# Order of set-up work in a fused attention and feed-forward block: constants behind the first layer norms, two weight loads behind the first keys, and one half of a down product in each phase

## The chip, the cores and the metric

The kernel runs on one core of a Trainium2 chip. The metric is the device time of one execution in microseconds (us), as a median over runs. Times inside an execution are counted from the start of the profiled span. The engines are PE (TensorE: matmuls; PEld is its weight load), DVE (VectorE), ACT (ScalarE), POOL (GpSimd) and SP (SyncE, which here only issues DMAs). SBUF is the memory on the core, PSUM the eight banks into which PE accumulates.

## What is computed

A transformer block on x of 2048 tokens by 448: layer norm, attention with 16 heads of 28 in a sliding window of 256, an output projection, a residual; then layer norm, a gated feed-forward part of width 1792, and a residual.

```python
q, k, v = layernorm(x) @ wqkv          # 16 heads of 28
p = softmax(where(0 <= i - j < 256, q @ k.T * 28 ** -0.5, -1e9))
h = x + (p @ v) @ wo
n = layernorm(h)
out = h + (gelu(n @ w_gate) * (n @ w_up)) @ w_down
```

## The kernel before

**Precision.** Matrix products of projections, values, output and feed-forward are made from float32 values split into a high half (rounded to the matmul's own float32 form) and a low half (the rest). One product tile is eleven matmuls, listed in TERMS: seven with the high half of the weights (against high and low halves of the tokens), four with the low half. `to_hi` (line 318, ACT) and `to_lo` (line 321, DVE, sometimes POOL) make the halves; lines 318 and 321 of the profile are these two helpers, so a piece is known by its tiles: `xT` for normed, transposed tokens, `proj` for weight tiles and for the halves of projected queries and keys, `wos` for wo, `rk` and `rq` for keys and queries as the scores read them.

**Who sets the order.** Nothing is scheduled by a compiler. `Lists.op` records every piece of work with its engine, a planned cost and latency, a key (its due time) and what it reads and writes; `after` adds pieces that it must wait for. `Lists.run` then plays the whole kernel through in planned time: at each step every engine takes, among the pieces that could start at once, the one with the smallest key, and the pieces are issued in that order. So each engine's queue is a fixed list, worked off in order on the chip, and one changed key or wait moves pieces everywhere behind it. Pieces with `port=True` on DVE and POOL are kept from overlapping in the plan.

**Opening.** `start` (line 420) loads four tiles of 128 tokens, the value weights of the first half (`wv_load(0)`), the first two weight tiles of queries and keys (`wqk_load`), the other twelve token tiles, and two more weight tiles. It makes the constants: `e8` and from it the picks (four pieces of `rk`, lines 474 to 480), zeros in rows 64 to 95 of `rq` and `rk` (lines 468 to 472), which two SBUF to SBUF copies repeat for the second block (lines 481 and 484), the mask (`const_mask`, line 449), and ones beside the values. `layer_norms` (line 333) makes per tile statistics on DVE (348, 350), a small chain on POOL (339 to 345), the norm `xn` on ACT (363), a transposition on PE (368) into a bank, then the high (318) and low (321) half of `xT`. `values` (line 504; matmuls in line 509) and `project_tile` (line 532; matmuls in 543) follow. While PE would idle early in the plan, `idle` puts in transpositions of `ident` that nobody reads (line 1041).

**Queries and keys** go through DRAM: the high and low half of a projected tile are made in one of two pairs of buffers (`pk`), stored by SP (lines 553 and 555), and loaded again in another layout by `loads` (line 575) for each block B of four query tiles and four heads. Scores are made twice: once for the row maxima (592, DVE 596), then, with the maxima as extra rows, for the exponentials (663, ACT 667); POOL cuts them to the window (678), PE weighs the values (697), and `drain` and `output` (741) finish. `wo_weights` (line 747) loads a part of wo into one raw buffer, splits it on ACT and POOL; it is called for both halves of a half of the heads as soon as the first projections are recorded. `wv_load(1)` loads the second half of the value weights.

**Feed-forward.** There are 56 products n, one per part of 128 of the width and per 512 tokens, in groups of 3, 4, 4 and 3 parts. The first four run as whole matmuls (869). From n = 4 on (PAIRED) a product runs in two phases of ten and eleven pairs of matmuls; a pair uses the upper and the lower half of PE's rows at the same time (845), and in the second phase the halves change sides. Between the phases a word of the bank is read by ACT (`seen`, line 851), which keeps PE from writing the bank too early. Then come gelu on ACT (907), the multiplication on DVE (909) and the halves of the result. The down product of n is also made in two halves of six pairs each, `down_a` and `down_b`, with two more such words behind `down_a`. At the end of a group DVE adds four banks to the residual (940). The order on PE is written out at the end of `feed_forward` (lines 822 to 835): four halves first, then phases and halves alternate.

## Time and profile before

| what | value |
|---|---|
| time, median of 3 runs | 742.24 us (741.76 to 743.04) |
| time of the profiled execution | 741.5 us |
| its span in the profile | 739.8 us |
| instructions | 15325 |
| bytes moved by DMA | 79.46 MB |
| paired feed-forward matmuls from xT and one weight record (L845) | 656 for 94.4 us, 393 ns each |
| projections (L543) | 308 for 97.3 us, 399 ns each |

Busy time of an engine is a share of the span; matmuls are pipelined, so their own durations overlap and a busy PE can still wait a little at each start. A row of a timeline gives start, duration, engine, line, operation, tiles and count, and in brackets the idle time before it and what ended it. A row with a count covers several instructions of one kind and the short gaps between them. A row of stretches gives for each engine busy time and count, the granted clock of PE, DMA's share and GB/s.

### The profile page before, as it was taken

The page shows a single profiled execution, that of the slowest core. Times are in us where ns is not written, and L with a number is a line of the kernel's source. Part 1 is how long each engine was busy: PE and PEld are TensorE (multiplying, and loading weights), DVE is VectorE, ACT ScalarE, POOL GpSimd, SP SyncE. Part 2 cuts the span into 40 slices and gives each one's busy share as a digit, 9 for nine tenths or more (in the row PEclk, how much of TensorE's full clock was granted, in tenths as well). Part 3 has the DMA queues.
Part 4 walks back from the last instruction along what each step waited for, and adds up shares of the span by engine and source line. Part 5 has one row for each costly group of instructions (what it writes and reads, how often), then busy time and mean ns, then how long its engine had stood idle before and what let it go on. Part 6 is the DMA issues. An engine that isn't in the chain of part 4 may idle for free.

```text
span 739.8 us, 15325 instructions
## 1 busy us (share of the span) xinstructions
PE 727.5 (98%) x5908; PEld 650.4 (88%) x5908; DVE 400.1 (54%) x1055; ACT 362.9 (49%) x929; POOL 154.2 (21%) x248
## 2 busy tenths in 40 slices
PE   8999999999999999999999999999999999999997
PEld 7787878888888787778899999999999999999996
DVE  8767977776677878848954413224433132223323
ACT  6657777667666888876643322223422122222221
POOL 5402544353344556463000000000000000000000
PEclk9999999999999999999999999999999999999999
DMA  9996536655565787516750200000100000001102
GB/s 280 260 306 204 169 121 200 192 184 158 166 184 179 185 237 204 134 42 177 166 162 1 87 38 1 1 2 1 42 2 1 1 1 2 1 1 51 51 1 101
DMA packets 83191, 79.46 MB, mean 107 GB/s; under 512 B 34126, under 2 KB 72974, under 8 KB 83086
## 3 DMA queue, kind: packets, MB, share of 16 engines
q1 hardware_dynamic: 83118, 78.48, 36.6%
q8 instruction: 46, 0.75, 0.4%
q14 instruction: 27, 0.22, 0.1%
HBM read 48.23 MB, written 29.36 MB: 105 GB/s over the span
## 4 chain that ended last, share of the span: by engine, by line
PE 88%; DVE 4%; ACT 3%; DMA 2%; issue 1%; SPq 1%; POOL 0%; DVEq 0%; ACTq 0%
PE bank L845 51%; PE bank L543 8%; PE bank L663 6%; PE bank L592 6%; PE bank L697 5%; PE bank L509 4%; PE bank L741 4%; PE bank L869 2%; DMA xT<-xn 1%; DVE bnst L348 1%; ACT pp L667 1%; DMA hres<-in_x_dram 1%; DVE xT L321 1%; ACT xn L363 1%; ACT xT L318 1%
## 5 line engine op out<-in xcount | busy, mean ns | idle before, releaser
L667 ACT ACTIVATE pp<-bank 128x384 f32<-128x384 f32 (+2 forms) x352 | 121.9, 389 | 52.1 <-PE bank L663 48.3
L596 DVE CUSTOM_DVE_ANT_0 mt<-bank,mt 128x384 bf16<-128x384 f32 (+2 forms) x256 | 127.6, 525 | 35.3 <-PE bank L592 33.0
L909 DVE TENSOR_TENSOR mt<-bank,mt 128x512 f32<-128x512 f32 x54 | 37.2, 690 | 169.7 <-ACT mt L907 169.5
L907 ACT ACTIVATE mt<-bank 128x512 f32<-128x512 f32 x54 | 32.1, 594 | 144.9 <-PE bank L845 144.9
L678 POOL TENSOR_SCALAR_AFFINE_SELECT pp<-pp 128x512 f32<-128x512 f32 x120 | 75.8, 644 | 126.5 <-ACT pp L667 122.4
L663 PE MATMUL bank<-rq,rk 104*128 104x384 f32 (+2 forms) x352 | 96.8, 304 | 1.4 <-ACT rq L318 0.7
L543 PE MATMUL bank<-xT,proj 128*128 128x512 f32 x308 | 97.3, 399 | 0.2 <-DVE bnmv L350 0.2
L845 PE MATMUL bank<-xT,rec 64*128 64x512 f32 x656 | 94.4, 393 | 0.0
L845 PE MATMUL bank<-xT,rk 64*128 64x512 f32 x656 | 91.3, 388 | 0.0
L845 PEld LDWEIGHTS bank<-xT,rec 64*128 64x128 f32 x656 | 81.1, 184 | 2.6
L845 PEld LDWEIGHTS bank<-xT,rk 64*128 64x128 f32 x656 | 79.5, 184 | 2.0
L592 PE MATMUL bank<-rk,rq 84*128 84x384 f32 (+2 forms) x256 | 81.0, 342 | 0.0
L663 PEld LDWEIGHTS bank<-rq,rk 104*128 104x128 f32 x352 | 64.3, 189 | 17.7 <-ACT pp L667 3.8
L851 ACT ACTIVATE word<-bank 1x1 f32<-1x1 f32 x162 | 25.8, 160 | 99.4 <-PE bank L845 96.4
L845 PE MATMUL bank<-xT,proj 64*128 64x512 f32 x533 | 72.7, 388 | 0.0
L845 PEld LDWEIGHTS bank<-xT,proj 64*128 64x128 f32 x533 | 63.0, 184 | 2.5 <-ACT word L851 0.4
L543 PEld LDWEIGHTS bank<-xT,proj 128*128 128x128 f32 x308 | 55.9, 189 | 6.3 <-ACT proj L318 0.4
L509 PE MATMUL bank<-proj,xT 128*128 128x224 f32 x352 | 59.7, 278 | 0.5 <-ACT xT L318 0.2
L845 PE MATMUL bank<-rk,proj 64*128 64x448 f32 x384 | 57.6, 362 | 0.0
L321 DVE TENSOR_TENSOR proj<-mt,proj 128x512 fp32r<-128x512 f32 x54 | 37.4, 692 | 35.7 <-ACT proj L318 35.6
L845 PE MATMUL bank<-rec,proj 64*128 64x448 f32 x360 | 54.3, 364 | 0.0
L509 PEld LDWEIGHTS bank<-proj,xT 128*128 128x128 f32 x352 | 52.3, 191 | 2.1 <-ACT xT L318 0.5
(114 smaller groups left out, 1155.6 us busy)
## 6 DMA issues: line engine op xcount, KB each, us to landing
rk<-k SPq DMA_DIRECT2D x44, 336.0 KB
rq<-q SPq DMA_DIRECT2D x32, 336.0 KB
q<-proj SPq DMA_DIRECT2D x16, 448.0 KB
k<-proj SPq DMA_DIRECT2D x12, 448.0 KB
raw<-in_ffn_dram SPq DMA_DIRECT2D x7, 736.0 KB
v<-in_ffn_dram SPq DMA_DIRECT2D x7, 736.0 KB
hres<-in_x_dram SPq DMA_DIRECT2D x16, 224.0 KB
q<-proj SPq DMA_DIRECT2D x16, 224.0 KB
```

The costliest lines, as they stand in the source:

```text
L321: (eng or nc.vector).tensor_sub(dst, src, f(hi))
L509: op("pe", mm(224), 0.29, key + a / 16, lambda a=a, h=h, wb=wb, xb=xb: nc.tensor.matmul(bank[b.k][:, 0:224], xT[:, xb, t * 128:(t + 1) * 1 ...
L543: op("pe", mm(512) + 0.002, 0.403, key, lambda a=a, h=h, wb=wb, xb=xb: nc.tensor.matmul(bank[b.k], wqk[i][:, h, wb, :], xT[:, xb, c * 512: ...
L592: nc.tensor.matmul(bank[b.k][:, o:384], rq[u][0:3 * DH, j, i * 128:i * 128 + 128], rk[u][0:3 * DH, j, m0 * 128:(i + 3) * 128], start=True, ...
L596: nc.vector.tensor_tensor_reduce(junk[s % 2][:, o:384], bank[b.k][:, o:384], mask[:, o:384], 1.0, -BIG, OP.add, OP.max, mx[i // 2][:, i % ...
L663: nc.tensor.matmul(bank[b.k][:, 0:n], rk[u][0:104, j, m * 128:m * 128 + 128], rq[u][0:104, j, lo * 128:(hi + 1) * 128], start=True, stop=True)
L667: nc.scalar.activation(pp[:, j, o * 128:o * 128 + n], bank[b.k][:, 0:n], AF.Exp, scale=SCALE)
L678: nc.gpsimd.affine_select(a, a, pattern=[[0, 4], [-cm, 128]], compare_op=op_, fill=0.0, base=0, channel_multiplier=cm)
L697: nc.tensor.matmul(bank[b.k][32 * j:32 * j + DH + 1, lo * 128:(hi + 1) * 128], v[:, 4 * c - 2 + m, g % 2, j, :], pp[:, j, at[m] * 128:(at[ ...
L845: nc.tensor.matmul(bank[bk.k][:, 0:n], w, m, start=bool(start), stop=bool(stop), tile_position=(64 * x, 0), skip_group_check=True)
L907: op("act", 0.485 + table, 0.608 + table, key + NP, lambda: nc.scalar.activation(blocks(g2), src(0), AF.Gelu_apprx_tanh), held[0], G2, bs[ ...
L909: op("dve", 0.605, 0.702, key + 2 * NP, lambda: nc.vector.tensor_tensor(blocks(g2), src(1), blocks(g2), op=OP.mult), [*G2, *held[1]], G2, ...
```

## The change

1. Constants. The zeros of `rk` and `rq` on POOL, the four picks, the two copies and the mask move from `start` into a function `constants`, called when the first four tiles' norms are recorded. All but the copies (which depend on the others) wait for the last piece of the fourth tile's norm, the low half of its `xT`.
2. Loads. `wo_weights` of the first half of the heads, and `wv_load(1)`, wait for the last load of block 1's keys. `wo_weights` is called after the loads of the second block of a half instead of before those of the first.
3. Down halves. Behind every phase of a product there is now one half of a down product. Before, there were two behind the first phase of product 4 alone, and from there on one.

```diff
-    def dma(key, size, fn, r=(), w=(), cost=0.44):
-        return op("sp", cost, 0, key, fn, r, w, size=size)
+    def dma(key, size, fn, r=(), w=(), cost=0.44, after=()):
+        return op("sp", cost, 0, key, fn, r, w, size=size, after=after)
...
         for t in ts:
             normalise(t, key(t), kind)
+            marks["xT", t] = L.ops[-1]
...
+    def constants(after):
...
-        op("pool", 1.35, 1.4, -99, lambda: nc.gpsimd.memset(f(rk_m[64:96, 0:1536]), 0.0), (), [("zk", 0, 0)], port=True)
-        op("pool", 0.95, 1.0, -98, lambda: nc.gpsimd.memset(f(rq_m[64:96, 1024:2048]), 0.0), (), [("zq", 0, 1)], port=True)
+        op("pool", 1.35, 1.4, -99, lambda: nc.gpsimd.memset(f(rk_m[64:96, 0:1536]), 0.0), (), [("zk", 0, 0)], port=True, after=after)
+        op("pool", 0.95, 1.0, -98, lambda: nc.gpsimd.memset(f(rq_m[64:96, 1024:2048]), 0.0), (), [("zq", 0, 1)], port=True, after=after)
...
                 op("dve", 0.55, 0.54, -96 + j, lambda j=j, src=src: nc.vector.tensor_copy(rk[0][96:104, j], src),
-                   ["e8"], [("pick", 0, j)], port=True)
+                   ["e8"], [("pick", 0, j)], port=True, after=after)
...
-        op("pool", 1.0, 1.0, -18, const_mask, (), ["mask"], port=True)
+        op("pool", 1.0, 1.0, -18, const_mask, (), ["mask"], port=True, after=after)
...
     def wv_load(p, key):
         for i in range(2):
             dma(key, 224, lambda i=i: nc.sync.dma_start(wv_raw[p][:, 2 * i:2 * i + 2], wv_in[p][:, 2 * i:2 * i + 2]),
-                (), [WVRAW(p, 2 * i, 2)])
+                (), [WVRAW(p, 2 * i, 2)], after=[got[HOLDV]] if p else ())
...
             get(1, c, i, 2, 2 + i, key + 4 * i)
+        got[B] = L.ops[-1]
...
-        dma(key - 20, 224, lambda: nc.sync.dma_start(wo_raw, wo_in[g]), (), [WORAW])
+        dma(key - 20, 224, lambda: nc.sync.dma_start(wo_raw, wo_in[g]), (), [WORAW], after=[got[HOLDO]] if g < 2 else ())
...
             for ph in phase[m]:
-                order.append(ph)
-                for _ in range(2 if ph is phase[PAIRED][0] else 1):
-                    order.append(todo.pop(0))
+                order += [ph, todo.pop(0)]
...
+                if c == 0:
+                    constants([marks["xT", 3]])
...
             if c == 0:
                 if not p:
                     clear()
-                wo_weights(2 * p)
-                wo_weights(2 * p + 1)
             for B in (8 * p + 2 * c, 8 * p + 2 * c + 1):
                 loads(B)
+                if B % 8 == 1:
+                    wo_weights(2 * p)
+                    wo_weights(2 * p + 1)
```

`HOLDO` and `HOLDV` are 1. The first zeros of `rq` (DVE, line 468), those of `rk` on ACT (471), `e8`, `ident` and the ones stay in `start`.

More of the change, by code (lines that the diff above doesn't have):

```diff
@@ L45 @@
 SOON = 2
+HOLDO = 1
+HOLDV = 1
 PAIRED = 4
@@ L330, in block_kernel @@
     NP = len(TERMS)
+    marks = {}
     def layer_norms(ts, key, kind):
@@ L354, in layer_norms @@
         for t in ts:
+            marks["ve", t] = L.ops[-1]
+        for t in ts:
             normalise(t, key(t), kind)
+            marks["xT", t] = L.ops[-1]
     def normalise(t, key, kind):
@@ L468, in start, with const_mask @@
         op("dve", 1.1, 1.15, -99, lambda: nc.vector.memset(f(rq_m[64:96, 0:1024]), 0.0), (), [("zq", 0, 0)])
[L469 to L470 removed]
         op("act", 1.45, 1.55, -97, lambda: nc.scalar.activation(
             rk_m[64:96, 1536:3072], e8[64:96, 0:1].to_broadcast([32, 1536]), AF.Copy), ["e8"], [("zk", 0, 1)])
+        op("pool", 0.9, 0.95, -10, lambda: nc.gpsimd.memset(v[:, :, :, :, DH:DH + 1], 1.0), (), ["ones"])
+        wv_split(0)
+    def constants(after):
+        def const_mask():
+            nc.gpsimd.memset(mask, 0.0)
+            nc.gpsimd.affine_select(mask[:, 0:128], mask[:, 0:128], pattern=[[1, 128]], compare_op=OP.is_gt,
+                                    fill=-BIG, base=0, channel_multiplier=-1)
+            nc.gpsimd.affine_select(mask[:, 256:384], mask[:, 256:384], pattern=[[-1, 128]], compare_op=OP.is_ge,
+                                    fill=-BIG, base=0, channel_multiplier=1)
+        op("pool", 1.35, 1.4, -99, lambda: nc.gpsimd.memset(f(rk_m[64:96, 0:1536]), 0.0), (), [("zk", 0, 0)], port=True, after=after)
+        op("pool", 0.95, 1.0, -98, lambda: nc.gpsimd.memset(f(rq_m[64:96, 1024:2048]), 0.0), (), [("zq", 0, 1)], port=True, after=after)
         for j in range(4):
@@ L476, in start @@
                 op("dve", 0.55, 0.54, -96 + j, lambda j=j, src=src: nc.vector.tensor_copy(rk[0][96:104, j], src),
-                   ["e8"], [("pick", 0, j)], port=True)
+                   ["e8"], [("pick", 0, j)], port=True, after=after)
             else:
                 op("act", 0.75, 0.85, -96 + j, lambda j=j, src=src: to_hi(rk[0][96:104, j], src), ["e8"],
-                   [("pick", 0, j)])
+                   [("pick", 0, j)], after=after)
         dma(-20, 246, lambda: nc.sync.dma_start(f(rk_m[84:104, 3072:6144]), f(rk_m[84:104, 0:3072])),
@@ L485, in start @@
             [("zq", 0, i) for i in range(2)], [("zq", 1, i) for i in range(2)])
-        op("pool", 1.0, 1.0, -18, const_mask, (), ["mask"], port=True)
-        op("pool", 0.9, 0.95, -10, lambda: nc.gpsimd.memset(v[:, :, :, :, DH:DH + 1], 1.0), (), ["ones"])
-        wv_split(0)
+        op("pool", 1.0, 1.0, -18, const_mask, (), ["mask"], port=True, after=after)
     def wv_load(p, key):
@@ L563, in block @@
         return 2 * p + r % 2, r // 2
+    got = {}
     def loads(B):
```

6 lines of the change are left out of this document (removed).

## The prediction

> **What bounds the kernel now.** I read the page first (busy shares, slices, the chain that ended last), then PE's timeline, then those of the other engines where PE is not dense.
>
> ```profile
> PE 727.5 (98%) x5908; PEld 650.4 (88%) x5908; DVE 400.1 (54%) x1055; ACT 362.9 (49%) x929; POOL 154.2 (21%) x248
> PE   8999999999999999999999999999999999999997
> DMA  9996536655565787516750200000100000001102
> PE 88%; DVE 4%; ACT 3%; DMA 2%; issue 1%; SPq 1%; POOL 0%; DVEq 0%; ACTq 0%
> ```
>
> PE is the bound: 98% busy, 88% of the chain. 98% of 739.8 us leaves 12.3 us idle, so no change that leaves the matmuls alone can win more than those plus unneeded PE work. The one loose slice is the first, and there the DMA queue is full (the first three slices, 55 us, read 9). So I looked at the opening.
>
> ```profile
> 2.13 5.12 PE L1041 MATMUL bank<-ident 128*128 128x128 f32 x25 [2.13 <-POOL ident L443]
> 8.20 0.66 PE L368 MATMUL bank<-ident,xn 128*128 128x128 f32 x4 [0.95 <-ACT xn L363]
> 11.66 1.25 PE L509 MATMUL bank<-proj,xT 128*128 128x224 f32 x9
> 13.54 1.69 PE L509 MATMUL bank<-proj,xT 128*128 128x224 f32 x13
> 15.10 1.13 PE L509 MATMUL bank<-proj,xT 128*128 128x224 f32 x8
> 16.07 5.17 PE L543 MATMUL bank<-xT,proj 128*128 128x512 f32 x22
> ...
> 30.53 0.66 PE L368 MATMUL bank<-ident,xn 128*128 128x128 f32 x4 [0.66 <-ACT xn L363]
> 32.34 0.66 PE L368 MATMUL bank<-ident,xn 128*128 128x128 f32 x4 [0.38 <-ACT xn L363]
> ...
> 39.05 0.34 PE L592 MATMUL bank<-rk,rq 84*128 84x128 f32 x2
> ```
>
> Useful work starts with the first transposition at 8.20; the 25 L1041 before it only keep PE going. Values (L509) start at 11.66, projections at 16.07 after 9+13+8 = 30 value products, scores at 39.05. PE loses 0.66 and 0.38 us to late norms near 31.
>
> **The change part by part.** Matmuls, DMAs and vector work are the same in number; the changed program has only 18 L1041 fewer (26 for 44). Everything else is order.
>
> ```profile
> 1.99 2.88 DVE L476 CAST rk<-e 8x768 fp32r<-8x768 f32 x2
> 4.90 0.63 DVE L348 BATCH_NORM_STATS2 bnst<-hres 128x6 f32<-128x448 f32 x1
> ...
> 14.45 1.76 DVE L321 TENSOR_TENSOR xT<-bank,xT 128x384 fp32r<-128x384 f32 x4
> ...
> 17.14 0.59 DVE L348 BATCH_NORM_STATS2 bnst<-hres 128x6 f32<-128x448 f32 x1
> ...
> 20.19 0.59 DVE L348 BATCH_NORM_STATS2 bnst<-hres 128x6 f32<-128x448 f32 x1
> 20.81 0.69 DVE L321 TENSOR_TENSOR proj<-bank,proj 128x512 fp32r<-128x512 f32 x1
> ...
> 22.75 1.27 DVE L321 TENSOR_TENSOR proj<-raw,proj 128x512 fp32r<-128x512 f32 x2
> ```
> ```profile
> 2.77 1.68 POOL L469 MEMSET rk<- 32x1536 f32 x1
> 5.92 0.23 POOL L339 TENSOR_SCALAR bnve<-bnmv 128x1 f32<-128x1 f32 x1 [0.17 <-POOL rq L470]
> ```
> ```profile
> 6.92 0.58 ACT L318 ACTIVATE proj<-pp 128x448 fp32r<-128x448 f32 x1 [1.45 <-DMA pp<-in_wv_dram]
> 7.40 0.74 ACT L363 ACTIVATE xn<-hres,bnve 128x448 f32<-128x448 f32 x1
> ```
> ```profile
> 0.00:4.00 4.00, 1.87 (x9) 1.87 (x10) 2.92 (x3) 3.17 (x4) 3.06 (x15) 1.00 0.52 141
> 0.00:6.00 6.00, 3.87 (x18) 3.87 (x19) 4.86 (x6) 4.64 (x5) 4.90 (x17) 1.00 0.67 187
> ```
>
> *1. Constants leave the head.* Now DVE's two picks (to 4.87) delay the first statistics to 4.90, and POOL's memsets delay L339 to 5.92 (its releaser is L470). The tile was there sooner: the stretch to 4.00 moved 4 x 141 = 564 KB (the last column is GB/s), and a tile has 229. So I start the first statistics at 3.4 instead of 4.90. Behind them it took 5.92 - 4.90 = 1.0 to POOL, 1.5 to the norm (7.40) and 0.8 to PE (8.20): now POOL about 4.3 (no memset in the way), the norm 5.6, the first transposition 6.4. The fourth tile gains less: four tiles are 917 KB, and the stretch to 6.00 moved 1122, so it lands near 5.5 and its statistics end about 0.6 earlier. From 6.92 ACT and DVE bound: ACT alternates weight halves, norms and high halves of xT at 0.5 to 0.65 us each, and DVE makes four low halves of 0.88 (1.76 for two tiles) and three of 0.6 in between. DVE can start at about 9.1 (6.92, three pieces of ACT and the first high half's own 0.6) and ends at 9.1 + 4 x 0.88 + 3 x 0.6 = 14.4; before, the 1.76 us from 14.45 end at 16.2. PE then starts values near 10.3 and, with 33 of them at 0.12 (1.69 for 13, less the last one's tail) and 0.5 for a transposition, projections at 14.8. That is 1.3 earlier than 16.07 with three more values done (0.35): **1.6 us ahead**.
>
> *2. They come back behind tile 3.* The constants now wait for the last low half (14.4). On POOL two memsets (1.68 for the larger) and the mask stand in front of the next norms, some 4 us; PE wants those only behind 40 projections and 14 values more, at 25: covered. On ACT two picks lie in a wait for PE: covered. On DVE it is tight. Behind 14.4 the changed order has both picks, seven statistics (20.19 - 17.14 over four: 0.76 each), two low halves of projections (0.69) and then the low half of the third weight tile (1.27 for two: 0.64). A pick alone is unknown: 1.44 each in the row, but they ran beside POOL's memsets, and the second ended at 4.87, 0.42 behind the larger memset (2.77 + 1.68). If it stood still until then, a pick takes 0.42. Bounds 0.42 and 1.44; I take 0.55, since the changed order puts POOL's and DVE's pieces mostly one behind the other. 14.4 + 1.1 + 5.3 + 1.4 + 0.64 = 22.85. PE reaches the first product that needs it (the eighth of its tile) at 14.8 + 29 x 0.23 (5.17 for 22) + 0.35 = 21.8 and waits 1.05. Before, that half was ready at 22.75 + 0.64 = 23.4 and PE did not wait. So 0.55 of the lead is left, plus the values: **0.9**. With picks of 1.44 it is 24.6, and 0.9 is lost instead.
>
> [...]
>
> *3. Loads moved behind the keys.*
>
> ```profile
> 12.74 0.91 SPq L481 DMA_DIRECT2D rk<-rk  x1
> ...
> 24.36 0.89 SPq L493 DMA_DIRECT2D raw<-in_wv_dram  x2
> ...
> 26.29 0.92 SPq L750 DMA_DIRECT2D raw<-in_wo_dram  x1
> ```
> ```profile
> 31.04 0.60 ACT L318 ACTIVATE proj<-bank 128x512 fp32r<-128x512 f32 x1 [0.57 <-DMA k<-proj]
> ```
>
> Now two loads of values and one of wo stand on SP (1.8 us of issue) between the stores of the first keys and their loads, in a full queue. ACT waits at 31.04 for such a store to land, the norms wait behind it, and PE loses the 0.66 + 0.38 quoted, with small change 1.3. The changed order has the fifth tile's transposition earlier and no such load among the stores. Against it, the copy rk<-rk, issued at 12.74 now, can go only after the second pick, about 19.5, straight in front of the first store. I take 0.3 of the stalls as left: **1.0 gained**; 1.3 at best, a loss of 1.0 if that copy holds the first store. Scores follow at about 37 instead of 39.05. The moved loads then fall into the fourth slice, where DMA has room (6). Their splits are not free.
>
> ```profile
> 24.27 1.16 POOL L321 TENSOR_TENSOR wos<-raw,wos 128x448 fp32r<-128x448 f32 x1 [1.96 <-ACT wos L318]
> ```
>
> This and its twin now stand among POOL's mask selections of the first block, 1.16 each; values wait for these. Bounds 0 and 2.3; nearer nothing, since PE has projections to do: **0.3 lost**.
>
> *4. One half of a down product per phase.*
>
> ```profile
> 354.51 1.59 PE L845 MATMUL bank<-rq,proj 64*128 64x448 f32 x12 [1.05 <-ACT word L851]
> ```
>
> At one place both halves of a down product stand back to back, and the second waits for ACT's one-word read of the first, itself late behind ACT's queue: 1.05 us idle. A phase of the next product, 22 matmuls, now stands between. What is late next is the word of the phase before, read by the same ACT queue with one half as cover instead of two: I allow 0.15. **0.9 gained**, bounds 0 and 1.05.
>
> Sum: 0.9 + 1.0 - 0.3 + 0.9 = **2.5 us**. In the profiled execution 741.5 (1.7 more than its span) becomes 739.0; the median of the runs shown is 0.74 higher, so 742.24 becomes **739.7**. Between 40 and 340 us the order of PE's rows is shuffled, with waits of tenths either way: plus or minus 1.
>
> **The rivals.** *A. DVE does not bind* (statistics overlap better than 0.76): 1.6 + 1.3 + 1.05 - 0.3 = 3.65, 738.6. Against it: the four statistics from 17.14 to 20.19 keep that pace with nothing between them.
>
> *B. The lead is given back*: long picks (-0.9), stalls as now (0), -0.3, +0.9: about 742.5, no change that a measurement can tell (under 0.2%, 1.5 us). For it: the pick's row, and the copy in front of the stores.
>
> *C. Slower: the wait moves to group ends.* There the four additions (L940) now come at the end of a product, in front of its multiplication.
>
> ```profile
> 621.62 0.69 DVE L909 TENSOR_TENSOR mt<-bank,mt 128x512 f32<-128x512 f32 x1 [5.16 <-ACT mt L907]
> ...
> 624.92 2.22 DVE L940 TENSOR_TENSOR hres<-bank,hres 128x448 f32<-128x448 f32 x4 [1.21 <-PE bank L845]
> ```
> ```profile
> 622.35 0.63 ACT L318 ACTIVATE proj<-mt 128x512 fp32r<-128x512 f32 x1
> 624.57 0.16 ACT L851 ACTIVATE word<-bank 1x1 f32<-1x1 f32 x1 [1.58 <-PE bank L845]
> ```
> ```profile
> 620.20 0.36 PE L845 MATMUL bank<-rk,proj 64*128 64x448 f32 x1
> ...
> 623.70 0.36 PE L845 MATMUL bank<-rk,proj 64*128 64x448 f32 x1
> ...
> 624.91 0.39 PE L845 MATMUL bank<-xT,proj 64*128 64x512 f32 x1
> ...
> 625.32 0.36 PE L845 MATMUL bank<-rk,proj 64*128 64x448 f32 x1
> ```
>
> The additions start 1.22 after their half (623.70). That half now stands where 620.20 is: 621.42 + 2.22 + 0.69 + 0.63 = 624.96. ACT's order has the high half in front of the word, so the word ends at 625.1 instead of 624.73, and the next phase, which started at 624.91, about 0.4 late. Fifteen group ends: 6 us, 745.7. Against it: the other half of the array is behind anyhow (it still runs the down product at 625.32, so its phase starts at about 625.5), which absorbs 0.4; it decides only if the word ends beyond about 625.3.
>
> *D. PE stays at half speed longer.* The 25 of the first row take 0.2 each, later ones less (13 values in 1.69). If fewer of them leave the clock low until about 16, 6 us of work doubles in price: 3.1 lost, 742.8. [...]
>
> **How the numbers follow.** Forecast 0.48; A 0.20; B 0.17; C 0.07; D 0.05; shuffled waits on the wrong side 0.03. The range goes from A with 1 us of shuffle and no loss at the wo splits, 737.3, to D, 742.8, and leaves out C. Faster by over 0.2% (under 740.8): the forecast nearly whole and A, 0.66; within: B and D nearly whole, and the forecast's edge, 0.24; slower: C and the rest, 0.10.
>
> **What would show it.** First statistics at 3.4, first transposition at 6.4, first projection near 14.8, a wait of PE for DVE's low half at 21.8 to 22.9, the first score at 37, no idle of 1.05 at the third product's second half, words behind high halves at group ends without idle time of PE. I am wrong if PE waits longer at 22, if the first stores land later than the copy lets them, or if a product's cycle grows.

## The result, and the profile after

| kernel | median | lowest to highest | runs |
|---|---|---|---|
| before | 742.08 us | 740.49 to 743.79 | 8 |
| changed | 744.35 us | 743.43 to 745.86 | 8 |

The ratio is 1.0032, 95% interval 1.0018 to 1.0046: the change makes the kernel 2.3 us slower. The forecast was 739.7, with a range to 742.8. The profiled execution took 743.81 us over a span of 742.1, against 741.5 over 739.8.

The page of the changed kernel, first, third and seventh of its busy lines, then the chain that ended last:

```profile
PE 727.5 (98%) x5890; PEld 652.2 (88%) x5890; DVE 398.7 (54%) x1055; ACT 364.7 (49%) x929; POOL 154.4 (21%) x248
PE   8999999999999999999999999999999999999997
DMA  8797556665656788615840210000100000001002
PE 89%; ACT 3%; DVE 3%; DMA 2%; issue 1%; SPq 0%; DVEq 0%; ACTq 0%
```

PE is busy exactly as long as before, 727.5 us, though it issues 18 transpositions fewer. So by the page the whole difference is idle time of PE, a few tenths at many places, and the page cannot show where. PE's timeline can (lines of the changed kernel are 2 to 14 higher than before; L375 is the transposition, L519 the values, L553 the projections, L605 the scores):

```profile
6.37 1.12 PE L375 MATMUL bank<-ident,xn 128*128 128x128 f32 x4
...
15.20 5.17 PE L553 MATMUL bank<-xT,proj 128*128 128x512 f32 x22
20.21 0.49 PE L519 MATMUL bank<-proj,xT 128*128 128x224 f32 x3
20.54 4.57 PE L553 MATMUL bank<-xT,proj 128*128 128x512 f32 x18
...
28.01 0.66 PE L375 MATMUL bank<-ident,xn 128*128 128x128 f32 x4 [0.65 <-ACT v L320]
29.14 0.65 PE L375 MATMUL bank<-ident,xn 128*128 128x128 f32 x4 [0.48 <-ACT xn L370]
...
32.38 0.66 PE L375 MATMUL bank<-ident,xn 128*128 128x128 f32 x4 [0.45 <-ACT xn L370]
...
38.05 0.22 PE L605 MATMUL bank<-rk,rq 84*128 84x128 f32 x1
```

The opening came as forecast up to 25 us: first transposition 6.37 (6.4), first projection 15.20 (14.8; before 16.07). Then three waits of 0.65, 0.48 and 0.45 stand between 28 and 33, where before had 0.66 and 0.38, and the first score comes only 1.0 earlier.

To compare whole stages I added up, over PE's matmuls, the time from one start to the next beyond the shortest that a matmul of that shape shows in the traces. This is PE's lost time; it shows what waits of under 0.2 us add up to, and is good to some 0.3 us, since a few records are missing. From the profiled executions, in us:

```
stage               20-55   55-100   100-345   345-400
before               4.62     5.30     21.08      1.70
changed              5.15     6.95     20.63      2.18
```

The changed kernel loses 0.5 us more in the opening, **1.65 more between 55 and 100**, and 0.5 more at the start of the paired feed-forward; between 100 and 345 it is 0.45 better, and from 360 on the two run alike. About 0.25 of the last two differences comes from where the stages are cut: one wait of PE for DVE stands at 344.90 in the kernel before and at 346.39 in the changed one. That is 2.2 us more, of which the lead at 20 us (about 1.1) covers half: the last matmul ends 1.5 us later (737.3 against 735.9; 0.4 of it these sums do not find). Another 0.8 us lies behind it: the span ends 4.75 us behind the last matmul instead of 3.93. In the experiments below that end took 3.9 to 4.8 us, and 4.7 to 4.8 in three of them (e5, e7, e10); what sets it is not shown.

PE's own waits from 38 to 345 us name the middle stage (columns: total, times, longest), before and then changed:

```profile
PE bank L663 <- ACT rq L318: 0.7, 1, 0.7
PE bank L663 <- ACT pp L667: 0.3, 1, 0.3
```
```profile
PE bank L605 <- DVE mx L609: 1.5, 3, 0.7
PE bank L676 <- ACT rq L320: 0.7, 1, 0.7
```

PE now waits 1.5 us for row maxima of DVE, which it never did before. The reason is beside those waits, in the timelines of DVE and POOL in the changed kernel:

```profile
74.09 1.27 DVE L625 TENSOR_SCALAR mhl<-mx 128x8 fp32r<-128x8 f32 x1
82.46 0.63 DVE L628 SCALAR_TENSOR_TENSOR mhl<-mx,mhl 128x8 fp32r<-128x8 f32 x1
```
```profile
74.06 1.28 POOL L323 TENSOR_TENSOR ohl<-oT,ohl 128x512 fp32r<-128x512 f32 x1 [0.32 <-ACT ohl L320]
82.44 0.64 POOL L691 TENSOR_SCALAR_AFFINE_SELECT pp<-pp 128x512 f32<-128x512 f32 x1 [1.27 <-ACT pp L680]
```

`mhl` is the small piece of DVE (8 columns) that negates the maxima; alone it lasts 0.17. Here it lasts 1.27 and 0.63: it starts 0.02 to 0.03 us behind a long piece of POOL and ends when that ends (74.06 + 1.28 = 75.34; 74.09 + 1.27 = 75.36). The kernel's plan keeps such pieces (`port=True`) apart, but in planned time; on the chip the pieces have moved by tenths. In the kernel before, POOL stretches only one small piece ahead of 150 us, at 106.0, to 0.31 us.

### The profile page after: what moved, and what is told of

The parts are those of the page before. It is cut to its first block, busy times and chain, and to the rows that moved or that the text cites. A ratio compares the mean times of both kernels' runs of the same rounds, so it can differ in the third digit from the quotient of the medians.

```text
span 742.1 us, 15355 instructions
## 1 busy us (share of the span) xinstructions
PE 727.5 (98%) x5890; PEld 652.2 (88%) x5890; DVE 398.7 (54%) x1055; ACT 364.7 (49%) x929; POOL 154.4 (21%) x248
## 3 DMA queue, kind: packets, MB, share of 16 engines
q1 hardware_dynamic: 83118, 78.48, 37.1%
## 4 chain that ended last, share of the span: by engine, by line
PE 89%; ACT 3%; DVE 3%; DMA 2%; issue 1%; SPq 0%; DVEq 0%; ACTq 0%
PE bank L856 51%; PE bank L553 9%; PE bank L676 7%; PE bank L605 6%; PE bank L710 5%; PE bank L754 4%; PE bank L519 4%; PE bank L880 2%; DVE xT L323 1%; DMA v<-in_ffn_dram 1%; ACT pp L680 1%; DMA pp<-in_wv_dram 1%; DVE bnst L352 1%; PE bank L375 1%; DMA k<-proj 1%
## 5 line engine op out<-in xcount | busy, mean ns | idle before, releaser
L553 PE MATMUL bank<-xT,proj 128*128 128x512 f32 x308 | 100.5, 402 | 0.0
L856 PE MATMUL bank<-xT,rec 64*128 64x512 f32 x656 | 89.0, 393 | 0.0
L856 PE MATMUL bank<-xT,rk 64*128 64x512 f32 x656 | 86.7, 388 | 0.0
L605 PE MATMUL bank<-rk,rq 84*128 84x384 f32 (+2 forms) x256 | 82.5, 343 | 1.7 <-DVE mx L609 1.5
L856 PEld LDWEIGHTS bank<-xT,rec 64*128 64x128 f32 x656 | 76.1, 185 | 3.7 <-ACT word L862 0.3
L856 PEld LDWEIGHTS bank<-xT,rk 64*128 64x128 f32 x656 | 76.9, 184 | 1.7
L856 PE MATMUL bank<-xT,proj 64*128 64x512 f32 x533 | 68.5, 388 | 1.1 <-ACT word L862 1.1
L951 DVE TENSOR_TENSOR hres<-bank,hres 128x448 f32<-128x448 f32 x64 | 35.4, 616 | 59.9 <-PE bank L856 52.6
L320 ACT ACTIVATE proj<-mt 128x512 fp32r<-128x512 f32 x54 | 34.1, 632 | 65.5 <-DVE mt L920 57.0
L856 PEld LDWEIGHTS bank<-xT,proj 64*128 64x128 f32 x533 | 60.6, 184 | 3.1 <-ACT word L862 1.4
L553 PEld LDWEIGHTS bank<-xT,proj 128*128 128x128 f32 x308 | 56.0, 190 | 6.2 <-ACT xn L370 0.3
L519 PE MATMUL bank<-proj,xT 128*128 128x224 f32 x352 | 58.5, 279 | 0.1
L605 PEld LDWEIGHTS bank<-rk,rq 84*128 84x128 f32 x256 | 47.2, 190 | 9.6 <-DVE mx L609 4.0
```

Of the source, the lines that this page charges most:

```text
L519: op("pe", mm(224), 0.29, key + a / 16, lambda a=a, h=h, wb=wb, xb=xb: nc.tensor.matmul(bank[b.k][:, 0:224], xT[:, xb, t * 128:(t + 1) * 1 ...
L553: op("pe", mm(512) + 0.002, 0.403, key, lambda a=a, h=h, wb=wb, xb=xb: nc.tensor.matmul(bank[b.k], wqk[i][:, h, wb, :], xT[:, xb, c * 512: ...
L605: nc.tensor.matmul(bank[b.k][:, o:384], rq[u][0:3 * DH, j, i * 128:i * 128 + 128], rk[u][0:3 * DH, j, m0 * 128:(i + 3) * 128], start=True, ...
L856: nc.tensor.matmul(bank[bk.k][:, 0:n], w, m, start=bool(start), stop=bool(stop), tile_position=(64 * x, 0), skip_group_check=True)
L951: op("dve", 0.533, 0.626, key + 2 * NP + 3 * q + 3, lambda t=t, b=down[q]: nc.vector.tensor_tensor(hres[:, t, :], bank[b.k][:, 0:D], hres[ ...
```

## The experiments

My theory after these views: (1) the moved copy rk<-rk, now in front of the first stores, takes the lead of the opening; (2) in the shuffled order POOL's long pieces hold up small pieces of DVE, in a stretch where DVE has little idle time, and PE pays; (3) the halves of the down products win nothing, because another wait stands right behind the one removed. The rivals: any new order costs PE its waits; the group ends; the clock. Times of before are medians of its runs on the same chip, taken with the experiment.

### Each part of the change alone

`e1_constants` is the kernel before with part 1 of the change, `e2_loads` with part 2, `e3_downs` with part 3, each by the lines of the diff above.

> The kernel before with the constants behind tile 3 alone (loads and down halves as before). Theory: the constants bring PE about 1 us ahead by the first projection, but the copy rk<-rk now stands in front of the first stores, so ACT waits 3 us or more for a store to land near 27 and the lead at the first score is under 0.7 us; the time is within 1 us of the kernel before. My recorded sum without the loads: 0.9 us faster, no wait of ACT above 1 us near 27. Rival (the order behind 40 us is what decides, and any change of it costs): slower by 1 to 3 us, with the loss between 40 and 340 us.

> The kernel before with the moved loads alone (constants in the head, down halves as before). Theory: with the copy back at 12.7 the stalls near 31 shrink, the first score comes 0.5 to 1.3 us earlier than 39.05, but the low halves of wo on POOL now stand between 55 and 75, pieces of POOL and DVE meet, and single small pieces of DVE (0.17 us) last 0.6 to 1.3 us, with PE waiting for row maxima 1.5 us in all: 0 to 1 us slower than before. Recorded step: 0.7 us faster, no such stretched pieces. Rival (DVE's stretched pieces have nothing to do with wo): no more of them than in the kernel before.

> The kernel before with one half of a down product in every phase alone. Theory: nothing changes before 340 us; PE's idle time of 1.05 at the third paired stretch stays in size and only stands ahead of the second phase of product 4, behind ACT's word, which stands behind a split that waits for a load of weights; the time is within 0.5 us of before. Recorded step: 0.9 us faster. Recorded rival C: 0.4 us lost at each of 15 group ends, 6 us slower.

| kernel | median (runs) | before | ratio, 95% interval |
|---|---|---|---|
| e1_constants | 747.61 (6) | 742.18 | 1.0073, 1.0045 to 1.0100 |
| e2_loads | 743.22 (12) | 742.18 | 1.0013, 1.0001 to 1.0025 |
| e3_downs | 743.35 (12) | 742.18 | 1.0008, 0.9994 to 1.0021 |

No part alone wins anything, and the three do not add up: 5.4, 1.0 and 1.2 us alone, 2.3 together. **e1** did what I expected in the opening: ACT waits 3.55 us for a store at 26.27 (6.1 in two waits), and the first score, at 38.47, is 0.6 earlier than before. The time missed, 5.4 us over before where I had expected at most 1. It has another source as well, which I had put down as a rival in the prediction only for the opening. PE's timeline, and the stretches with PE's granted clock (third column from the end):

```profile
51.56 0.44 PE L676 MATMUL bank<-rq,rk 104*128 104x384 f32 x1 [1.00 <-ACT rq L320]
52.44 0.73 PE L553 MATMUL bank<-xT,proj 128*128 128x512 f32 x2 [0.43 <-ACT v L320]
...
360.14 2.27 PE L858 MATMUL bank<-rq,proj 64*128 64x448 f32 x12 [2.36 <-ACT word L864]
```
```profile
52.00:54.00 2.00, 1.57 (x8) 1.48 (x8) 1.20 (x5) 1.27 (x5) 0.00 (x0) 0.84 0.64 205
54.00:56.00 2.00, 2.00 (x7) 1.81 (x7) 0.51 (x4) 0.89 (x3) 0.00 (x0) 0.50 0.82 256
56.00:58.00 2.00, 2.00 (x11) 1.78 (x10) 1.00 (x5) 1.20 (x4) 1.23 (x2) 0.80 0.03 10
360.00:363.00 3.00, 2.86 (x16) 2.42 (x18) 1.96 (x5) 2.97 (x9) 0.00 (x0) 0.59 0.49 83
```

Behind waits of 1.00 and 0.43 us, and again behind one of 2.36, the clock fell to a half for 3.4 us: 7 matmuls between 54 and 56 where 11 stand at 56 to 58. Each time costs about 1.7 us on top of the wait, an estimate from half of 3.4. Five of its six runs have a mean clock under 0.999; the sixth took 744.97, so some 3 us are lost without the clock. The constants alone are the worst of the three, with the old loads of wo and the values still among the stores; that those loads make the difference is not shown.

**e2** has its first score at 36.46, 2.6 us before the kernel before (with less done; I had expected 0.5 to 1.3), and one small piece of DVE 0.87 us too long at 60.2, beside a low half of wo on POOL, as expected. But PE has no wait for row maxima between 55 and 100, where I had expected 1.5 us. It loses another 0.5 us between 100 and 345. **e3** moved no time that 12 runs can tell. PE's idle time at 354, which I had expected to stay, was gone in its execution, and this stood in its place (PE, then SP):

```profile
371.41 0.50 PE L854 MATMUL bank<-xh,proj 64*128 64x512 f32 x1 [0.77 <-DMA xh<-xT]
```
```profile
365.71 0.42 SPq L793 DMA_DIRECT2D v<-in_ffn_dram  x1
366.25 0.47 SPq L828 DMA_DIRECT2D xh<-xT  x1
```

The copy of 128 KB that PE needs was issued behind a weight load of 736 KB, which landed at 370.7; the copy landed at 371.4, 5.1 us after its issue. Rival C, 0.4 us at 15 group ends, is refuted: neither e3 nor the changed kernel has a wait at any group end.

### The copies behind the first stores

`e4_copies` is the changed kernel with the two copies in a function of their own, called behind `project` of the first tiles:

```diff
+            if not p and c == 0:
+                copies([marks["put", 1]])     # the last store of the second projected tile
```

> The changed kernel, with its two copies rk<-rk and rq<-rq issued behind the stores of the second projected tile instead of ahead of the first stores. Theory: ACT's wait of 4.28 us for a store at 27.11 shrinks to under 1.5, PE's waits between 25 and 33 shrink from 1.6 to about 0.7, and the first score comes at about 37.1 instead of 38.05; if that lead is kept the time is 0.9 us under the changed kernel, about 743.4. Rival (the stores are late because the queue is full anyway): the wait stays above 3 us and the first score at 38. Rival (a lead at 38 is given back later): the first score at 37 and the time as the changed kernel's.

743.19 us (12 runs; before 742.18), ratio 1.0007 (0.9994 to 1.0019): 1.2 under the changed kernel. What ACT waited for between 20 and 34 us in the changed kernel (then PE's waits from 25 to 34) is quoted here; in e4 ACT's list has no store in it, and PE's list is empty.

```profile
ACT proj L320 <- DMA k<-proj: 5.3, 2, 4.3
ACT proj L320 <- PE bank L553: 1.2, 1, 1.2
```
```profile
PE bank L375 <- ACT xn L370: 0.9, 2, 0.5
PE bank L375 <- ACT v L320: 0.7, 1, 0.7
```

The theory holds for ACT's wait: it was the copy, not a queue that is full anyway. The first score came at 36.38, earlier than the 37.1 expected, but PE had waited 1.27 for it, with nothing else ready.

### POOL behind DVE's small pieces

`e5_behind` is the changed kernel, `e8_before_behind` the kernel before, `e12_loads_behind` e2, each with a read of one column ahead of POOL's long pieces. There are 40 such copies in the traces of e5 and 39 in e8's, not 56 as the expectations say.

```diff
+    def behind():
+        if small:                             # (k, column) that DVE's last small piece wrote
+            k, c = small.pop()
+            nc.gpsimd.tensor_copy(word[:, 8:9], f(mhl[k][:, c:c + 1]))
...
+            behind()
             a = pp[:, :, o * 128:o * 128 + 128]
```

> The changed kernel with 56 one-column copies on POOL, each ahead of a selection or another long piece of POOL, that read what DVE's last small piece of the maxima (0.17 us each) wrote, so that POOL starts only behind that piece. The order of everything else is the changed kernel's. Theory (POOL's long pieces hold DVE's small ones up where DVE is nearly full, and PE waits for the row maxima behind them): no such small piece of DVE between 40 and 100 us lasts over 0.4 us (there are pieces of 1.27 and 0.63 now), PE's three waits of 1.5 us for row maxima go below 0.5, and the time falls by 0.8 to 1.7 us, to 742.7 to 743.5. Rival (DVE is simply late with the maxima): the pieces get short, PE's waits stay above 1 us, and the time is within 0.5 us of the changed kernel's.

> The kernel before with the same 56 one-column copies on POOL, its order unchanged. In it no small piece of DVE is held up before 150 us, and from there on 3.3 us in all, where DVE has room. Theory: the copies themselves cost nothing and there is nothing on PE's path to win: within 0.5 us of the kernel before. Rival (each held-up piece costs PE its stretch): 1 to 3 us faster. If the waits that the copies put on POOL delay selections: slower by 0.5 us or more.

> The kernel before with the moved loads alone, and the 56 one-column copies on POOL. Theory: of the 1 us that the moved loads cost, the meeting of POOL and DVE at 60.2 (a small piece 0.86 us longer, PE 0.7 us idle behind) goes, and the time is 0.5 to 1 us under that of the loads alone, 742.2 to 742.7. Rival (the losses between 110 and 180 us decide): no change against the loads alone, 743.2.

| kernel | median (runs) | before | ratio, 95% interval | lost 55-100 |
|---|---|---|---|---|
| e5_behind | 742.85 (12) | 742.14 | 1.0006, 0.9993 to 1.0018 | 5.79 |
| e8_before_behind | 741.80 (11) | 742.14 | 0.9994, 0.9984 to 1.0005 | 5.50 |
| e12_loads_behind | 742.67 (11) | 741.89 | 1.0001, 0.9986 to 1.0015 | 6.01 |

**e5** gave what the theory asked: 1.5 us off the changed kernel (the two intervals of the ratio just touch, at 1.0018). DVE and POOL in it, at the place that is quoted above:

```profile
74.84 0.17 DVE L632 TENSOR_SCALAR mhl<-mx 128x8 fp32r<-128x8 f32 x1
```
```profile
75.15 0.18 POOL L624 COPY word<-mhl 128x1 f32<-128x1 f32 x1 [0.66 <-DVE mhl L632]
75.29 1.27 POOL L323 TENSOR_TENSOR ohl<-oT,ohl 128x512 fp32r<-128x512 f32 x1
```

POOL waits 0.66 us, which costs nothing, the small piece lasts 0.17, and PE's waits for maxima shrink from 1.5 to 0.4. A piece of 0.58 stays at 76.0, so one meeting is left. **e8** says that the copies themselves cost nothing. It does not say what the meetings behind 150 us cost, for most of them are still there: what small pieces of over 0.3 us last beyond 0.17 is 2.3 us in all, against 2.6 before. **e12** is inside its range, but its small piece at 60.5 is still 0.87 too long (POOL's piece stood ahead of it in the queue), so it does not tell the two readings apart.

### The weight loads behind the copies xh<-xT

`e6_hold` is e3 with the loads of parts 4 and later held back in the plan; `e9_hold_warm` adds 13 transpositions of ident that nobody reads, and `e11_before_warm` is the kernel before with these 13 alone.

```diff
+        for o in late[4:]:                    # loads of weights, in order of parts
+            for d in xhs:                     # the four copies xh<-xT
+                o.deps.add(d)
+                d.users.append(o)
```
```diff
         def tr():
+            for _ in range({0: 8, 1: 5}.get(t, 0) if kind == "ln1" else 0):
+                nc.tensor.transpose(bank[b.k][:, 0:128], ident, ident)
```

> The kernel before with one half of a down product per phase, and with the loads of the weights of parts 4 and later issued behind the four copies xh<-xT. With the halves alone the idle 1.05 us near 354 went, but PE then waited 0.77 us at 371.4 for a copy xh<-xT that was issued at 366.25 behind a weight load of 0.75 MB and landed at 371.37. Theory (the gain of the halves was real, and a transfer behind a weight load took it back): neither wait is left, and the time is 0.7 to 1.3 us under the kernel before. Rival (something else catches PE next, the norms of the later tokens): a wait of 0.5 us or more stays between 350 and 400, and the time is within 0.5 us of before.

> The kernel before with one half per phase and the weight loads behind the copies xh<-xT, and with 13 more transpositions of ident that nobody reads, 8 ahead of the first tile's and 5 ahead of the second's. Without them 10 of 11 runs showed a mean clock below 1.000 and the profiled one a clock of 0.5 from 9 to 12 us behind 2.67 us of idle time. Theory (the 1.3 us won at 354 was there, and a clock halved behind idle time in the opening hid it): most runs show a clock of 0.999 or more and the time is 0.7 to 1.5 us under the kernel before. Rival (nothing was won): within 0.4 us of the kernel before with the same transpositions.

> The kernel before with the 13 more transpositions alone. Theory: about a third of its runs show a clock under 0.999 and take 1.6 us longer; with them gone the median falls by 0.3 to 0.6 us. Rival (no part in the clock): the same share of runs under 0.999 and the same median.

| kernel | median (runs) | before | ratio, 95% interval | lost 345-400 |
|---|---|---|---|---|
| e6_hold | 742.97 (11) | 742.14 | 1.0007, 0.9995 to 1.0020 | 1.18 |
| e9_hold_warm | 742.27 (11) | 741.89 | 0.9998, 0.9982 to 1.0014 | 1.18 |
| e11_before_warm | 743.14 (11) | 741.89 | 1.0011, 0.9996 to 1.0026 | 2.24 |

In the stage both waits are gone, as the theory has it: e6 and e9 have one wait of 0.3 us left between 346 and 400. In the whole time I missed: e6 was to be 0.7 to 1.3 under before and is 0.8 over it, e9 was to be 0.7 to 1.5 under and is 0.4 over. e6's profiled execution lost 1.8 us more than before in the first 20 us, though the program there is the same:

```profile
9.27 1.11 PE L375 MATMUL bank<-ident,xn 128*128 128x128 f32 x4 [2.67 <-ACT xn L370]
```
```profile
8.00:10.00 2.00, 0.73 (x4) 0.73 (x5) 0.81 (x3) 2.00 (x4) 1.73 (x4) 0.68 1.01 380
10.00:12.00 2.00, 2.00 (x11) 2.00 (x10) 1.25 (x3) 1.85 (x4) 1.43 (x6) 0.50 1.05 401
```

The first weight load landed at 7.96 instead of 6.89, the first norm behind it came late, PE idled 2.67 us, and the clock fell. 7 of e6's 11 runs have a mean clock under 0.999; with the transpositions 1 of 11 (e9) and none of 11 (e11). So the transpositions do keep the clock up, but e11 was no faster for it, against its theory; why its median is 1.2 us over before is open (its first weight load landed at 8.41 in the one execution seen). e9 is 0.9 under e11, so what it loses less than e11 between 345 and 400 (1.1 us) may be a gain in time too; against the kernel before, neither e6 nor e9 shows one.

### All mends at once

`e7_all` is the changed kernel with e4's, e5's and e6's edits; `e10_all_warm` adds 3, 10 and 5 transpositions ahead of the first three tiles'; `e14_wo_dve` is that with the low halves of wo on DVE instead of POOL.

> The changed kernel with three mends at once: the copies rk<-rk and rq<-rq behind the stores of the second projected tile, POOL's pieces behind DVE's small ones, and the weight loads of parts 4 and later behind the copies xh<-xT. Theory: the mends add up, 1.1 us for the copies, 0.8 to 1.5 for the meetings of POOL and DVE, 1 for the weight loads: 740.7 to 741.7, 0.5 to 1.5 us under the kernel before. Rival (whatever lead PE has in the opening is lost to waits by 180 us): faster than the changed kernel by the weight loads' 1 us alone beside the copies, about 742.2, no better than before.

> The changed kernel with the three mends, and with 18 more transpositions of ident, 3 ahead of the first tile's, 10 ahead of the second's, 5 ahead of the third's. Theory: the mean clock is 0.999 or more in most runs, where it was in 4 of 12, and the median goes from 741.7 to 740.5 to 741, 1 to 1.6 us under the kernel before. Rival (the clock's low stretches lie elsewhere, or the idle time in the opening has no part in them): clocks and time as without them. If they overrun the first tiles: projections later than 15.4 and a time of 742 or more.

> The changed kernel with all mends and the 18 transpositions, and with the low halves of wo on DVE (about 0.6 us each) instead of POOL (1.15 each). In the kernel without this a small piece of DVE lasts 1.07 us beside POOL's low half of wo at 61.5, and PE loses 6.9 us between 55 and 100. Theory (that meeting is the rest of the loss): no small piece over 0.7 us near 62, 5.4 to 6.2 us lost in the stretch, and 740.3 to 741.2. Rival (DVE has no room there, and 1.2 us more work on it costs PE as much): the loss stays at 6.6 or more and the time at 741.5 or above.

| kernel | median (runs) | before | ratio, 95% interval | lost 55-100 |
|---|---|---|---|---|
| e7_all | 741.73 (12) | 742.14 | 1.0000, 0.9984 to 1.0016 | 6.98 |
| e10_all_warm | 741.55 (12) | 741.89 | 0.9993, 0.9979 to 1.0007 | 6.94 |
| e14_wo_dve | 741.61 (12) | 742.50 | 0.9987, 0.9972 to 1.0002 | 7.08 |

e7 is 2.6 us off the changed kernel and level with before: at the upper end of its theory. e10's transpositions brought the runs under 0.999 from 8 of 12 to 2 of 12 and the median down by only 0.2 us, against its theory of 0.7 or more. The lost time says why it is not more: with the copies moved, the order changes once more, and the stretch from 55 to 100 loses 7 us again. I put this on a small piece of DVE that still met POOL's low half of wo (1.07 us at 61.6 in e10). In e14 that meeting is gone and the loss is not: the rival was right. So a meeting need not cost PE anything: with the copies moved (e4, e7, e10), PE has no wait of 0.2 us or more for maxima between 60 and 100. What binds that stretch in this order is open.

### The changed order kept, three mends

`e13_order_kept` is the changed kernel with e5's reads, e6's loads and e10's transpositions, the copies left where the change has them; `e15_no_warm` is that without the transpositions, `e16_no_behind` without the reads.

> The changed kernel with POOL behind DVE's small pieces, the weight loads of parts 4 and later behind the copies xh<-xT, and 18 more transpositions of ident, but with the copies rk<-rk and rq<-rq where the changed kernel has them. By the profiles so far PE loses between 55 and 100 us 5.3 to 5.6 us in every kernel with the order of before, 7.0 in the changed one, 5.8 in it with POOL behind, 6.9 with the copies moved as well. Theory (what costs most is the meeting of POOL and DVE in that stretch): 5.6 to 6.0 lost there, no small piece of DVE over 0.7 us, and 740.5 to 741.2, about 1 us under the kernel before. Rival (the copies' 1.0 us at 27 weighs as much): 741.5 to 742, as the kernel before.

> The changed kernel with POOL behind DVE's small pieces and the weight loads behind the copies xh<-xT, without the 18 transpositions that the fastest kernel so far (739.89, all 7 runs at a clock of 0.999 or more) had besides. Theory (the transpositions only keep the clock up in some runs): runs at 0.999 or more take 739.5 to 740.6, a third or more of the runs show a lower clock and take about 1.5 us longer; median 740.2 to 741.2. Rival (the transpositions did the most): median 741.7 or above, with no gap between runs of either clock. Rival (they did nothing): 739.9 and no low clock.

> The changed kernel with the weight loads behind the copies xh<-xT and the 18 transpositions, but without POOL's reads of DVE's small pieces. Theory (the meetings of POOL and DVE cost about 1.2 us): pieces of 1.2 and 0.6 us near 74 and 83 are back, PE loses 6.8 to 7.1 us between 55 and 100 instead of 5.9, and the time is 740.9 to 741.7. Rival (the meetings cost nothing and the small copies changed something else): 739.6 to 740.4.

| kernel | median (runs) | before | ratio, 95% interval | lost 55-100 | lost 345-400 |
|---|---|---|---|---|---|
| e13_order_kept | 739.89 (7) | 742.50 | 0.9957, 0.9939 to 0.9974 | 5.94 | 0.37 |
| e15_no_warm | 740.85 (12) | 742.19 | 0.9980, 0.9969 to 0.9990 | 5.82 | 0.48 |
| e16_no_behind | 741.44 (11) | 742.19 | 0.9988, 0.9980 to 0.9997 | 6.94 | 0.44 |

e13 beats both kernels, and by more than expected (740.5 to 741.2). Its page, and PE's waits between 60 and 100 us in e13 and in e16:

```profile
PE 728.2 (99%) x5908; PEld 653.4 (89%) x5908; DVE 397.5 (54%) x1055; ACT 364.7 (49%) x929; POOL 160.4 (22%) x288
```
```profile
PE bank L607 <- DVE mx L611: 0.2, 1, 0.2
```
```profile
PE bank L607 <- DVE mx L611: 1.3, 2, 0.7
```

Taking the reads out brings back the pieces of 1.27 and 0.63 us, the 1.3 us of waits, 1.0 us of lost time in that stretch, and 1.55 us of time (the intervals of e13 and e16 lie apart). That is the same price as between the changed kernel and e5 (1.50), on another base. Theory 2 is shown for these two meetings: 1.0 to 1.2 of the 1.5 us lie in their stretch, and where the rest lies is not shown. The weight loads are worth 2.0 us (e5 to e15), more than the 0.7 lost less between 345 and 400. In the executions profiled the end behind the last matmul is 0.6 shorter (4.22 against 4.78), which need not come from the loads; the rest is not accounted for. The transpositions are worth about 1.0 on this base (e15 to e13), which neither e10 nor e11 showed on theirs. e15's profiled execution shows what they are for, once more the stretches with the clock:

```profile
10.00:12.00 2.00, 1.34 (x9) 1.11 (x8) 1.88 (x4) 1.73 (x4) 1.93 (x3) 0.83 1.06 399
12.00:14.00 2.00, 2.00 (x12) 2.00 (x10) 1.72 (x5) 1.81 (x4) 1.54 (x4) 0.50 1.04 376
```

6 of e15's 12 runs have a mean clock under 0.999, none of the 18 of e13 and e16. By the medians these six take 0.7 us longer than the other six, not the 1.5 that I had expected.

## Why the prediction was wrong, step by step

The sum was 0.9 + 1.0 - 0.3 + 0.9 = 2.5 us faster. Only the first term, the opening, came nearly so. The second failed because the copy held the first stores, the last because a wait of the same size stood one phase later, and the order between 55 and 100 us cost 1.65 more, where I had allowed 1 for all shuffling and named no cause.

**Steps 1 and 2, the constants: right, with one slip.** First statistics at 3.32 (3.4), POOL's first piece 4.26 (4.3), norm 5.56 (5.6), transposition 6.37 (6.4), values 10.86 (10.3), first projection 15.20 (14.8) with the 33 values. That is 0.87 earlier and 0.35 of values, 1.2 ahead where I said 1.6. The picks took 0.56 each (0.55), and the low half of the third weight tile was ready at 23.37 (22.85). PE lost only about 0.4 there (the 18 projections at 20.54 take 4.57, not 4.2) instead of 1.05. The slip: I let POOL's memsets wait for tile 3. They and the mask ran at 9.44 to 12.8, ahead of it: `after` orders the plan, and a queue that nothing blocks runs ahead of the plan. It did no harm.

**Step 3, the loads: wrong, by the bound that I put aside.** I wrote 1.0 gained, "a loss of 1.0 if that copy holds the first store", and took the first. Measured, the stage from 20 to 55 us lost 0.5 more than before. SP and ACT in the changed kernel:

```profile
19.08 0.75 SPq L493 DMA_DIRECT2D rk<-rk  x1
19.93 0.43 SPq L565 DMA_DIRECT2D q<-proj  x1
20.41 1.85 SPq L565 DMA_DIRECT2D k<-proj  x1
```
```profile
27.11 0.60 ACT L320 ACTIVATE proj<-bank 128x512 fp32r<-128x512 f32 x1 [4.28 <-DMA k<-proj]
```

The copy went at 19.08, as I had it (19.5); the first store behind it landed at 24.2, 4.3 us after its issue, where before's took 3.6, and SP itself stood 1.85 us in the next issue. ACT's piece of the third tile then waited 4.28 us for a buffer that a store was still reading, and the norms of the next tiles wait behind ACT. e4 takes the copy away, and ACT's waits for stores and PE's between 25 and 34 us are gone. I had both numbers in front of me, the copy's time of issue and its place ahead of the first store, and treated the collision as a tail.

**POOL's pieces: 0.3 taken for the splits of wo, 1.2 to 1.5 measured, and by another way.** I asked which values wait for POOL. Nothing did. PE paid for small pieces of DVE that stood still beside a long one of POOL. In the two meetings that piece is a low half of the attention's output and a mask selection, not a split of wo; whether the moved splits brought them there is not shown (e2, the loads alone, has neither of the two meetings). That DVE's pieces can take more than twice as long beside POOL's was in my own row of the picks (1.44 each beside memsets, 0.56 alone now), and I used it at that one place only. The trace shows that the one stands still beside the other, with ends 0.02 us apart (75.36 behind 75.34), and does not show why.

**Step 4, the halves: the cycle was read rightly, the next wait was not.** I allowed 0.15 for the word of the phase before. In the changed kernel (PE, then ACT):

```profile
356.03 2.78 PE L856 MATMUL bank<-xT,proj 64*128 64x512 f32 x21 [1.05 <-ACT word L862]
```
```profile
355.30 0.63 ACT L320 ACTIVATE rk<-v 128x512 fp32r<-128x512 f32 x1 [1.03 <-DMA v<-in_ffn_dram]
355.83 0.14 ACT L862 ACTIVATE word<-bank 1x1 f32<-1x1 f32 x1
```

The word stands in ACT's queue behind a split of weights that PE first reads at 410.5, 55 us later, and that split waits 1.03 us for its load. So 1.05 us are idle as before, one phase later. In e3, e4 and e5, where that load came in time, 0.6 to 0.8 us went to a copy behind another weight load instead. Only with those loads held back (e6, e9, e13, e15, e16) is neither wait left in that stage.

**Shuffled order: plus or minus 1.** Between 100 and 345 us it was 0.45 better; between 55 and 100, 1.65 worse, two thirds of it the meetings (e5). My rival B, the lead given back, was nearest: it had the copy in front of the stores. But its long picks did not come (0.56 each), and it lacked the meetings. Of the chance of 0.10 that I gave to a slower kernel, 0.07 was for C, which did not happen.

**Rivals.** A (DVE does not bind) is not borne out: the statistics behind tile 3 do not overlap better than I had them (16.76, 17.56), and the low half they stand in front of came later than forecast; PE lost little there all the same, and that was worth nothing further on. C is refuted. D, the clock, is real, but mostly not as I had it: it fell again behind idle time, in the opening of both kernels (behind 2.67 us in e6, which has the opening of the kernel before, and behind 0.54 and 1.65 in e4 and 1.39 and 0.66 in e15, which have that of the changed one). A clock that stays low until about 16, and the 3.1 us for it, no run shows: in both kernels a transposition of `ident` lasts 0.42 us at first, and 0.27 from 8.7 on in the kernel before, from 9.3 on in the changed one. Nearest to it comes e7's profiled execution, where 31 matmuls kept PE busy for 7.12 of the first 10 us; in e5's 30 took 5.88. Of the 29 runs of the kernel before that were taken with e1 to e4, 11 had a mean clock under 0.999 and a median of 743.4, the others 741.9. It explains little of the 2.3 us: at 0.999 or more the changed kernel's median is 743.7 (4 runs).

What stays open: e11's median; the 7 us lost between 55 and 100 once the copies are moved; 1.3 of the 2.0 us that the weight loads brought on e5's base; the end behind the last matmul; and 0.5 to 1.5 us by which single executions of one order differ between 100 and 345 us.

## What to carry to other kernels

When a transfer is moved, look at what it is now in front of, and price the case in which it holds that up before the case in which it is hidden. A plan that keeps two engines apart in planned time did not keep them apart on the chip (POOL's piece at 74.06, DVE's at 74.09 in the changed kernel): where it matters, let the engine with slack wait for the other on a real result (40 reads of 0.18 us on POOL were worth 1.5 us here). A wait that is removed is a gain only if what the next instruction needs is already there; ask it of every queue that stands behind, ACT's and SP's too, and hold back big loads that nobody needs yet.

## What the runs showed of the chip

A small piece of DVE (128 by 8) that started while a long piece of POOL ran ended 0.02 to 0.03 us behind it: it took 1.27 us at 74.09 and 0.63 at 82.46 in the changed kernel, and 1.07 at 61.62 in e10, instead of 0.17. One that started ahead of POOL's piece kept its length (0.16 us at 153.13 in the changed kernel, POOL's piece starting at 153.18).

PE's clock fell to a half for 3.4 us at a time, behind pairs of idle times of 1.00 and 0.43 us (e1), 0.54 and 1.65 (e4), 1.39 and 0.66 (e15), and behind single ones of 1.85 (e12), 2.36 (e1) and 2.67 us (e6). But the length of one idle time does not decide: it stayed at 1.00 behind 1.71 (e5), 2.15 (e7) and 2.49 us (e8). What decides a fall is not shown.

An SBUF to SBUF copy of 240 KB in 20 rows, issued at 19.08, was landed only at 23.6, and the five stores issued between 19.93 and 23.36 landed 4.0 to 4.5 us after their issue; the first six stores of the kernel before took 2.4 to 3.6.
